# Attention and mixture of experts: five late slots of three blocks, early buffers, and the next x turned in quarters

## The chip, the cores and the metric

The kernel runs on one core of a Trainium2 chip. The time is the device time of one execution, in microseconds, taken as the median of several runs. The profile is of one further execution; its engines are TensorE (PE, with PEld for the loading of the stationary operand), VectorE (DVE), ScalarE (ACT), GpSimd (POOL) and SyncE (SP), which issues most of the DMA transfers.

## The reference

An attention over 32 memory rows a head makes x, and a mixture of eight experts works on x. Each token goes to the one expert with the largest gate logit.

```python
a = softmax(phi, axis=sequence)              # batch 8, heads 8, sequence 576, memory 32
k_m, v_m = a^T k, a^T v                      # per head: 32 x 64
attn = softmax(q k_m^T / 8) v_m              # 8 x 8 x 576 x 64
x = attn as 4608 tokens x 512
e_idx = argmax(x @ w_gate)                   # 512 x 8
out[t] = prob[t, e] * sigmoid(x @ w_output_gate)[t, e] * (relu(x[t] @ w1[e]) @ w2[e])
                                             # w1: 8 x 512 x 1024, w2: 8 x 1024 x 512
```

Everything is float32. The counts of tokens of the experts follow from the data, and the kernel finds them at run time.

## The kernel before

**Attention.** The eight batches are worked as four pairs. For each pair a generator `memory` makes the memory rows (18 pauses long in its written order MEM), and the queries go in five chunks a pair, 20 in all. The loop over `t` in `attention` does one step for each chunk, and some more for its lag: the list ORDER says in which order the parts of a step are issued, and each part works on the chunk that its lag gives. X is the exponential (ACT, L796), S the transpose, the maximum and the shift (DVE L787 and L790, POOL L792), D the division, B the transpose back, V0 and V1 the values (PE L825, copy on ACT L827, store on SP L936 and L940), C the scores of the next chunk (PE L779), M and m a pause's worth of `memory`, R a number of pauses of the routing. Each engine works its instructions in the order in which they are issued here.

**Routing.** After each pair, `rank` finds the expert of each token and its place among that expert's tokens. After the second pair `route_early(0)`, after the third `route_early(1)`, after the last `route_late` turn counts into a plan of slots. A slot is up to three blocks of 128 tokens of one expert. Two plus three early slots of three (NPS) take full triples only; then come NPT late slots of three, NPP of two, and up to NSS of one, which run in branches only if the counts ask for them (`used`). A slot's expert is in the table `slot` (read by SP), its rows in the lists `idx_ga`, `idx_gb` (slots 2 to 4) and `idx_gl` (the late ones), DVE L238. `known` marks slots whose expert is there, `listed` those whose rows are.

**Experts.** `run` works the slots in order. The rows are gathered from `xs` in HBM (POOL L480), turned by TensorE against the identity into a PSUM bank (`turn_x`, L988), and split into a high part (ACT L989) and a low part (DVE L990). A slot's weights are eight units of 512 KB: four of w1 (L1117), four of w2 (L1136). Each is loaded (SP L507) into a buffer of the ring `raw`, and split into high (ACT L518) and low (DVE L519) into the ring `ring`. Every product is taken three times (high by high, low by high, high by low). Relu and its split are ACT L1122 and DVE L1123, the scaled result ACT L1096, its scatter POOL L1097. After each unit, `done` splits as many units ahead as the ring allows.

**How the two are interleaved.** At the part S of step 19 (START) the slots begin, and the rest of the attention and the late routing are issued from `hook` in `several`, two entries of ORDER or two pauses at a time: twice a unit in u=0 to 3, and once for each block of a unit in u=4 to 7. Before the slots begin the rings have three raw buffers, two split ones and one for gathered rows. `grow(0)` adds two to each, in memory that the attention's pools `qk` and `ld` leave when they are closed; `grow(1)` adds the rest after slot 1 (LAST, `settle`). PSUM has four banks for the slots until then, and six afterwards; the results of w2 hold three of them from u=4.

Of the kernel before, what the change touches and what calls it, by code (L numbers as in the profile page):

```python
# [7 lines left out]
F32 = mybir.dt.float32  # L8
# [4 lines left out]
ALU = mybir.AluOpType  # L13
# [3 lines left out]
P = 128  # L17
B, H, S, D, M = 8, 8, 576, 64, 32
# [7 lines left out]


NPS = (2, 3)
NPT, NPP, NSS = 6, 4, 19
NPE = sum(NPS)  # L30
NB3, NB2 = 3 * NPT, 2 * NPP
NBL = NB3 + NB2 + NSS
NSLOT = NPE + NPT + NPP + NSS
NTHR = 13

ORDER = ["R4", "X", "S", "R0", "m", "D", "M", "B", "V0", "R1", "R1", "V1", "M", "m", "C"]
LAG = {"X": 1, "B": 2, "D": 1, "V": 3, "C": -1}
TICK = 0
HOOK = (2, 2, 2, 2, 2, 2)
# [13 lines left out]
LATE = {"lg": 8, "w": 2, "pe": 0, "dve": 0}  # L53
GROW = ((2, 2, 2), (6, 1, 0))
PUMP = (2, 1)
LAST = 1
XQ = 144
XROW = 4 * XQ
# [6 lines left out]
def attention_moe(tc, phiT, kv, qT, wgo, wall, out):  # L65
    nc = tc.nc
    V, A, G, T = nc.vector, nc.scalar, nc.gpsimd, nc.tensor

    with contextlib.ExitStack() as ctx:
# [5 lines left out]
        ident = cp.tile([P, P], F32, name="ident")  # L75
# [387 lines left out]
        for s in range(NSLOT):  # L463
            nb = 3 if s < NPE + NPT else 2 if s < NPE + NPT + NPP else 1
            if s < NPE:
                k = s >= NPS[0]
# [7 lines left out]
        order = slots  # L474
# [497 lines left out]
                    self.step()  # L972
                return self.got

        def turn_x(z, c2):

            nb, xg = z["nb"], z["xg"]
            if c2 == 0:
                z["x"] = (mo.tile([P, 4, 3 * P], F32R, name="xh"), mo.tile([P, 4, 3 * P], F32R, name="xl"))
            xh, xl = z["x"]  # L980
            n = nb * P
            w = 1 if nb == 3 else 2
            for c in range(2 * c2, 2 * c2 + 2, w):
                pt = bank([w, 512 // w], "ps")
                for j in range(w):
                    for k in range(nb):
                        o = (c + j) * XQ
                        T.transpose(pt[:, j, k * P:(k + 1) * P], xg[:, k, o:o + P], ident[:])  # L988
                A.copy(xh[:, c:c + w, 0:n], pt[:, :, 0:n])  # L989
                V.tensor_tensor(xl[:, c:c + w, 0:n], pt[:, :, 0:n], xh[:, c:c + w, 0:n].bitcast(F32), ALU.subtract)  # L990

        NT = 5 * NBP
        deferred = []
# [18 lines left out]
        def attention():  # L1012

            nonlocal rou
            st, lgs = {}, {}
            while 0 not in kTs:
                mem.step()
            st[0] = scores(0, 0)
            load_q(NQ)
            xo = None  # L1020
            for t in range(NT + LAG["V"]):
                for w in ORDER:
                    g = t - LAG.get(w[0], 0)
                    if w in ("M", "m"):
                        if w == "M" or t % 5 < 4:
                            mem.step()
                    elif w[0] == "R":
                        rou.step(int(w[1:]))
                    elif w == "W":
                        if order[0]["known"] and stream.parted < ring.size:  # L1030
                            stream.split(ring.size)
                    elif w == "V0" and 0 <= g < NT:
                        bp, c = g // 5, g % 5
                        while 2 * bp + (c >= 2) not in ves:
                            mem.step()
                        if g == 5 * bp:
                            lgs[bp] = rt.tile([P, NCH, 16], F32, name="lg", bufs=2)
                        xo = wk.tile([P, 2, 2, 2 * XQ], F32, name="xo", bufs=2)
                        values(bp, 2 * c, st[g], xo)
                    elif w == "V1" and 0 <= g < NT:  # L1040
                        if c < 4:
                            values(bp, 2 * c + 1, st[g], xo)
                        store(bp, c, xo, lgs[bp])
                    elif w == "C" and 0 < g < NT:
                        while 2 * (g // 5) + (g % 5 >= 2) not in kTs:
                            mem.step()
                        st[g] = scores(g // 5, g % 5)
                        if g + NQ < NT:
                            load_q(g + NQ)
                    elif w == "S" and 0 <= g < NT:  # L1050
                        shift(st[g])
                    elif w == "X" and 0 <= g < NT:
                        expo(st[g])
                    elif w == "D" and 0 <= g < NT:
                        divide(st[g])
                    elif w == "B" and 0 <= g < NT:
                        back(st[g])
                    undefer()
                    clock[0] += 1
                    yield "open" if w == "S" and t == START else None  # L1060
                g = t - LAG["V"]
                if g >= 0 and g % 5 == 4:
                    bp = g // 5
                    undefer(99)
                    left.append(bp)
                    rou.finish()
                    if bp < NBP - 1:
                        rou = Side(rank(bp, lgs[bp]))
                    else:
                        late.gens.append(rank(bp, lgs[bp]))  # L1070
                if t == NT - 1:
                    mem.finish()
                    pm.close()
                    grow(0)
# [26 lines left out]
        def several(i, st, nxt, hook):  # L1101

            z = order[i]
            nb, x, h = z["nb"], z["x"], []
            n_ = nb * P
            for u in range(4):
                w = st.take(i, u)
                h_ = mo.tile([P, 2, 3 * P], F32R, name="hh", bufs=4)
                l_ = mo.tile([P, 2, 3 * P], F32R, name="hl", bufs=4)
                for j in range(2):  # L1110
                    if nb == 3 or j == 0:
                        pb = bank([1, 512] if nb == 3 else [2, 256], "ps")
                    n = 0
                    for cc in range(4):
                        for a, b in PASS:
                            o = cc * 256 + j * P
                            T.matmul(pb[:, j % pb.shape[1], 0:n_], w[:, b, o:o + P], x[a][:, cc, 0:n_],  # L1117
                                     start=(n == 0), stop=(n == 11))
                            n += 1
                    if nb == 3 or j == 1:  # L1120
                        js = slice(j, j + 1) if nb == 3 else slice(0, 2)
                        A.activation(h_[:, js, 0:n_], pb[:, :, 0:n_], AF.Relu)  # L1122
                        V.scalar_tensor_tensor(l_[:, js, 0:n_], pb[:, :, 0:n_], 0.0, h_[:, js, 0:n_].bitcast(F32),  # L1123
                                               ALU.max, ALU.subtract)
                    if j == 0:
                        hook()
                h.append((h_, l_))
                st.done(PUMP[0])
                hook()
            py = [bank([DM], "ps") for _ in range(nb)]  # L1130
            for u in range(4, 8):
                w = st.take(i, u)
                for k in range(nb):
                    for f in range(2):
                        for n, (a, b) in enumerate(PASS):
                            T.matmul(py[k], h[u - 4][a][:, f, k * P:(k + 1) * P], w[:, b, DM * f:DM * f + DM],  # L1136
                                     start=(u == 4 and f == 0 and n == 0), stop=(u == 7 and f == 1 and n == 2))
                    if u == 7:
                        finish_y(z, k, py[k])
                    hook()  # L1140
                if u in (4, 6):
                    nxt(u // 2 - 2)
                st.done(PUMP[0])

        def single(i, st, nxt):
# [16 lines left out]
            for u in range(4):  # L1162
# [12 lines left out]
                    turn_h(0)  # L1175
                if u < 3:
                    st.done(PUMP[1])
            nxt(0)
            nxt(1)
            turn_h(1)  # L1180
            st.done(PUMP[1])
            py = bank([DM], "ps")
# [22 lines left out]
        def run(st):  # L1205

            lo, hi = st.lo, st.hi // 8
            while not order[lo]["known"]:
                force()
            st.fetch()  # L1210
            if lo:
                gat[:] = lo, hi

            def hook():
                gathers(i)
                clock[0] += not att.gens
                (att if att.gens else late).step(HOOK[min(i, 5)])

            for i in range(lo, hi):
                gathers(i, i + 1)  # L1220
                if i == lo:
                    turn_x(order[i], 0)
                    turn_x(order[i], 1)

                def nxt(c2):
                    if i + 1 < hi:
                        gathers(i, i + 2)
                        turn_x(order[i + 1], c2)

                if order[i]["nb"] > 1:  # L1230
                    several(i, st, nxt, hook)
                else:
                    single(i, st, nxt)
                if i == LAST:
                    settle()
# [56 lines left out]
```

## Time and profile before

| | us |
|---|---|
| median of 3 runs | 670.93 (670.58 to 672.78) |
| the profiled execution's own time | 669.65 |
| its span, first to last instruction | 667.9 |
| mean granted TensorE clock | 0.937 |
| TensorE busy | 587.3 (88%) |
| VectorE busy | 354.5 (53%) |
| ScalarE busy | 285.4 (43%) |
| GpSimd busy | 166.2 (25%) |

The span is cut by the first matmul on w1 (L1117) of each slot. Attention and early routing lie ahead of 130.3 us; the 15 slots follow up to about 652 us; the last scatters and the check for single slots end it. A row of a view of stretches gives the stretch, its length, and for each engine its busy time with the number of instructions, then the granted clock (1.00 is full), the busy share of the DMA engines and GB/s. A row of a timeline gives start, duration, engine, line, operation, tiles and shapes, and in brackets how long the engine was idle before and what ended that.

### The profile page before, as it was taken

How to read it: one execution, taken by the hardware profiler on the slowest of the kernel's cores; microseconds unless marked ns; L12 is line 12 of the kernel's file. 1: busy time of each engine (PE TensorE's matmuls, PEld its weight loads, DVE VectorE, ACT ScalarE, POOL GpSimd, SP SyncE). 2: the span in 40 equal slices, each digit the busy share in tenths (PEclk: the TensorE clock that was granted, in tenths of full speed). 3: DMA queues.
4: the chain of work that ended last, by engine and by line, in shares of the span. 5: the costliest groups of instructions: out<-in, count | busy, mean ns of one | idle time of the engine just before them, and what ended most of it. 6: DMA issues, size and time to landing. Idle time of an engine off the chain costs nothing. (4 is left out here: it accounts for less than half of the span.)

```text
span 667.9 us, 11253 instructions
## 1 busy us (share of the span) xinstructions
PE 587.3 (88%) x4287; PEld 505.7 (76%) x4287; DVE 354.5 (53%) x706; ACT 285.4 (43%) x479; POOL 166.2 (25%) x198
## 2 busy tenths in 40 slices
PE   4588886577699889989999999999999999999990
PEld 3356563466479679888989898989898999899880
DVE  3668799744345559954444444444445353565410
ACT  4556654323235246423434353535343444555410
POOL 2334656402401441120304040303020212121101
PEclk9889688578799999989999999999999999999996
DMA  8999999313555749554645555464746363776000
GB/s 313 411 399 409 380 346 307 110 53 104 183 172 172 242 111 340 191 144 147 197 155 172 181 156 196 140 213 108 233 114 201 126 190 119 230 245 180 22 6 26
DMA packets 42911, 129.25 MB, mean 194 GB/s; under 512 B 9824, under 2 KB 9888, under 8 KB 42464
## 3 DMA queue, kind: packets, MB, share of 16 engines
q1 hardware_dynamic: 36288, 106.90, 49.2%
q0 software_dynamic: 6560, 21.54, 8.9%
q8 instruction: 36, 0.59, 0.3%
q14 instruction: 27, 0.22, 0.1%
HBM read 108.07 MB, written 21.66 MB: 194 GB/s over the span
## 5 line engine op out<-in xcount | busy, mean ns | idle before, releaser
L1117 PE MATMUL bps<-xh,whl 128*128 128x384 f32 (+1 forms) x960 | 235.8, 329 | 10.1 <-ACT whl L518 6.1
L1136 PE MATMUL bps<-whl,hh 128*128 128x512 f32 x656 | 215.2, 398 | 2.2 <-ACT whl L518 1.5
L519 DVE TENSOR_TENSOR whl<-w,whl 128x1024 fp32r<-128x1024 f32 x120 | 145.4, 1225 | 88.2 <-ACT whl L518 88.2
L1117 PEld LDWEIGHTS bps<-xh,whl 128*128 128x128 f32 x960 | 171.6, 193 | 14.5 <-ACT whl L518 7.4
L1117 PE MATMUL bps<-xl,whl 128*128 128x384 f32 (+1 forms) x480 | 156.7, 326 | 0.0
L1136 PEld LDWEIGHTS bps<-whl,hh 128*128 128x128 f32 x656 | 124.1, 189 | 29.0 <-ACT whl L518 1.8
L1136 PE MATMUL bps<-whl,hl 128*128 128x512 f32 x328 | 128.8, 393 | 0.0
L518 ACT CAST whl<-w 128x1024 fp32r<-128x1024 f32 x120 | 123.7, 1049 | 0.0
L1122 ACT ACTIVATE hh<-bps 128x384 fp32r<-128x384 f32 (+1 forms) x104 | 52.0, 509 | 112.8 <-PE bps L1117 112.8
L1123 DVE SCALAR_TENSOR_TENSOR hl<-bps,hh 128x384 fp32r<-128x384 f32 (+1 forms) x104 | 58.7, 575 | 70.1 <-ACT hh L1122 69.9
L1117 PEld LDWEIGHTS bps<-xl,whl 128*128 128x128 f32 x480 | 92.9, 193 | 0.5
L1097 POOL DMA_INDIRECT out<-y,idx_ol x26 | 32.0, 1231 | 234.5 <-ACT y L1096 205.4
L990 DVE TENSOR_TENSOR xl<-bps,xh 128x384 fp32r<-128x384 f32 (+1 forms) x52 | 28.6, 575 | 95.6 <-ACT xh L989 95.4
L989 ACT CAST xh<-bps 128x384 fp32r<-128x384 f32 (+1 forms) x52 | 24.2, 498 | 123.7 <-PE bps L988 123.7
L1136 PEld LDWEIGHTS bps<-whl,hl 128*128 128x128 f32 x328 | 62.2, 190 | 11.6
L1096 ACT ACTIVATE y<-bps,xg 128x512 f32<-128x512 f32 x41 | 28.2, 688 | 61.6 <-DMA out<-y,idx_ol 23.8
L988 PE MATMUL bps<-ident,xg 128*128 128x128 f32 x164 | 26.6, 292 | 10.9 <-DMA xg<-xs,idx_ga 5.2
L825 PE MATMUL bpd<-ve_b,aT 64*128 64x144 f32 (+1 forms) x320 | 31.7, 358 | 4.0 <-DVE ea L787 2.4
L988 PEld LDWEIGHTS bps<-ident,xg 128*128 128x128 f32 x164 | 21.0, 148 | 16.7 <-DVE xl L990 5.6
L827 ACT COPY xo<-bpd 128x576 f32<-128x576 f32 x36 | 22.5, 637 | 25.7 <-PE bpd L825 16.1
L480 POOL DMA_INDIRECT xg<-xs,idx_gl x26 | 27.9, 1072 | 18.8 <-DVE idx_ol L241 11.2
L825 PEld LDWEIGHTS bpd<-ve_b,aT 64*128 64x128 f32 (+1 forms) x320 | 24.3, 218 | 10.2 <-DVE ea L787 3.1
(232 smaller groups left out, 427.4 us busy)
## 6 DMA issues: line engine op xcount, KB each, us to landing
w<-wall SPq DMA_DIRECT2D x120, 512.0 KB, 4.3
kvt<-kv SPq DMA_DIRECT2D x32, 512.0 KB, 7.9
xs<-xo SPq DMA_DIRECT2D x16, 576.0 KB, 5.7
qt<-qT SPq DMA_DIRECT2D x16, 512.0 KB, 8.3
ph<-phiT SPq DMA_DIRECT2D x3, 1152.0 KB, 12.0
kv<-kv SPq DMA_DIRECT2D x4, 512.0 KB, 9.2
ph<-phiT SPq DMA_DIRECT2D x4, 288.0 KB, 3.9
xs<-xo SPq DMA_DIRECT2D x8, 144.0 KB, 3.9
```

The lines of the kernel that those rows point to most:

```text
L480: G.indirect_dma_start(out=z["xg"][:, k], out_offset=None, in_=xs[0:z["rows"]], in_offset=bass.IndirectOffsetOnAxis(ap=z["idx"][0][:, q:q ...
L518: A.copy(hl[:, 0], w[:])
L519: V.tensor_tensor(hl[:, 1], w[:], hl[:, 0].bitcast(F32), ALU.subtract)
L825: T.matmul(px[to:to + n, r, sl], z["aT"][h, o:o + n], ves[2 * bp + b][h, g], start=True, stop=True)
L988: T.transpose(pt[:, j, k * P:(k + 1) * P], xg[:, k, o:o + P], ident[:])
L990: V.tensor_tensor(xl[:, c:c + w, 0:n], pt[:, :, 0:n], xh[:, c:c + w, 0:n].bitcast(F32), ALU.subtract)
L1096: A.activation(y[:], py, AF.Copy, scale=z["xg"][:, k, P:P + 1])
L1097: G.indirect_dma_start(out=out, out_offset=bass.IndirectOffsetOnAxis(ap=z["idx"][1][:, z["q0"] + k:z["q0"] + k + 1], axis=0), in_=y[:], in ...
L1117: T.matmul(pb[:, j % pb.shape[1], 0:n_], w[:, b, o:o + P], x[a][:, cc, 0:n_], start=(n == 0), stop=(n == 11))
L1122: A.activation(h_[:, js, 0:n_], pb[:, :, 0:n_], AF.Relu)
L1123: V.scalar_tensor_tensor(l_[:, js, 0:n_], pb[:, :, 0:n_], 0.0, h_[:, js, 0:n_].bitcast(F32), ALU.max, ALU.subtract)
L1136: T.matmul(py[k], h[u - 4][a][:, f, k * P:(k + 1) * P], w[:, b, DM * f:DM * f + DM], start=(u == 4 and f == 0 and n == 0), stop=(u == 7 an ...
```

## The change

Three things are edited.

- NPT goes from 6 to 5, and NSS from 19 to 22. The lists keep 45 columns.
- In the attention: W joins ORDER behind R4. The loop already has a branch for it, which splits one weight unit if slot 0 is known and fewer units are split than the ring has buffers. The edit adds a second branch with the same condition further down the same chain of `elif`. And the closing of the pools `qk` and `ld` with `grow(0)` goes from the end of step 19 to the end of step 18.
- `turn_x` now turns one quarter of the next slot's x (one chunk of 128 columns; two at once where the slot has fewer than three blocks), and `several` calls it at four places of its second half instead of two halves behind u=4 and u=6. TURN gives the places, counted in blocks of units from u=4: for three blocks 1, 4, 6 and 9 of 12.

```diff
--- before.py
+++ after.py
@@ -26,14 +26,14 @@
 
 
 NPS = (2, 3)
-NPT, NPP, NSS = 6, 4, 19
+NPT, NPP, NSS = 5, 4, 22
 NPE = sum(NPS)
 NB3, NB2 = 3 * NPT, 2 * NPP
 NBL = NB3 + NB2 + NSS
 NSLOT = NPE + NPT + NPP + NSS
 NTHR = 13
 
-ORDER = ["R4", "X", "S", "R0", "m", "D", "M", "B", "V0", "R1", "R1", "V1", "M", "m", "C"]
+ORDER = ["R4", "W", "X", "S", "R0", "m", "D", "M", "B", "V0", "R1", "R1", "V1", "M", "m", "C"]
 LAG = {"X": 1, "B": 2, "D": 1, "V": 3, "C": -1}
 TICK = 0
 HOOK = (2, 2, 2, 2, 2, 2)
@@ -53,6 +53,7 @@
 LATE = {"lg": 8, "w": 2, "pe": 0, "dve": 0}
 GROW = ((2, 2, 2), (6, 1, 0))
 PUMP = (2, 1)
+TURN = {3: (1, 4, 6, 9), 2: (1, 2, 4, 5)}
 LAST = 1
 XQ = 144
 XROW = 4 * XQ
@@ -972,22 +973,24 @@
                     self.step()
                 return self.got
 
-        def turn_x(z, c2):
+        def turn_x(z, c):
+
 
             nb, xg = z["nb"], z["xg"]
-            if c2 == 0:
+            if c == 0:
                 z["x"] = (mo.tile([P, 4, 3 * P], F32R, name="xh"), mo.tile([P, 4, 3 * P], F32R, name="xl"))
             xh, xl = z["x"]
             n = nb * P
             w = 1 if nb == 3 else 2
-            for c in range(2 * c2, 2 * c2 + 2, w):
-                pt = bank([w, 512 // w], "ps")
-                for j in range(w):
-                    for k in range(nb):
-                        o = (c + j) * XQ
-                        T.transpose(pt[:, j, k * P:(k + 1) * P], xg[:, k, o:o + P], ident[:])
-                A.copy(xh[:, c:c + w, 0:n], pt[:, :, 0:n])
-                V.tensor_tensor(xl[:, c:c + w, 0:n], pt[:, :, 0:n], xh[:, c:c + w, 0:n].bitcast(F32), ALU.subtract)
+            if c % w:
+                return
+            pt = bank([w, 512 // w], "ps")
+            for j in range(w):
+                for k in range(nb):
+                    o = (c + j) * XQ
+                    T.transpose(pt[:, j, k * P:(k + 1) * P], xg[:, k, o:o + P], ident[:])
+            A.copy(xh[:, c:c + w, 0:n], pt[:, :, 0:n])
+            V.tensor_tensor(xl[:, c:c + w, 0:n], pt[:, :, 0:n], xh[:, c:c + w, 0:n].bitcast(F32), ALU.subtract)
 
         NT = 5 * NBP
         deferred = []
@@ -1029,6 +1032,10 @@
                     elif w == "W":
                         if order[0]["known"] and stream.parted < ring.size:
                             stream.split(ring.size)
+                    elif w == "W":
+
+                        while t == NT - 1 and stream.split(2):
+                            pass
                     elif w == "V0" and 0 <= g < NT:
                         bp, c = g // 5, g % 5
                         while 2 * bp + (c >= 2) not in ves:
@@ -1068,7 +1075,7 @@
                         rou = Side(rank(bp, lgs[bp]))
                     else:
                         late.gens.append(rank(bp, lgs[bp]))
-                if t == NT - 1:
+                if t == NT - 2:
                     mem.finish()
                     pm.close()
                     grow(0)
@@ -1138,8 +1145,9 @@
                     if u == 7:
                         finish_y(z, k, py[k])
                     hook()
-                if u in (4, 6):
-                    nxt(u // 2 - 2)
+                    step = nb * (u - 4) + k
+                    if step in TURN[nb]:
+                        nxt(TURN[nb].index(step))
                 st.done(PUMP[0])
 
         def single(i, st, nxt):
@@ -1175,8 +1183,8 @@
                     turn_h(0)
                 if u < 3:
                     st.done(PUMP[1])
-            nxt(0)
-            nxt(1)
+            for c in range(4):
+                nxt(c)
             turn_h(1)
             st.done(PUMP[1])
             py = bank([DM], "ps")
@@ -1219,13 +1227,13 @@
             for i in range(lo, hi):
                 gathers(i, i + 1)
                 if i == lo:
-                    turn_x(order[i], 0)
-                    turn_x(order[i], 1)
-
-                def nxt(c2):
+                    for c in range(4):
+                        turn_x(order[i], c)
+
+                def nxt(c):
                     if i + 1 < hi:
                         gathers(i, i + 2)
-                        turn_x(order[i + 1], c2)
+                        turn_x(order[i + 1], c)
 
                 if order[i]["nb"] > 1:
                     several(i, st, nxt, hook)
```

## The prediction

> **What bounds the kernel now.** I read the page first, then TensorE's work in stretches cut at the first L1117 matmul of each slot, then its waits.
>
> ```profile
> span 667.9 us, 11253 instructions
> PE 587.3 (88%) x4287; PEld 505.7 (76%) x4287; DVE 354.5 (53%) x706; ACT 285.4 (43%) x479; POOL 166.2 (25%) x198
> ```
>
> ```profile
> core 0: us, PE busy (x) PEld busy (x) DVE busy (x) ACT busy (x) POOL busy (x), PEclk, DMA share, GB/s
> 130.26:198.77 68.51, 52.08 (x229) 41.28 (x229) 28.36 (x70) 19.13 (x29) 13.11 (x15) 0.83 0.39 121
> 198.77:240.29 41.52, 37.72 (x237) 32.76 (x235) 22.11 (x65) 16.63 (x27) 13.93 (x17) 1.00 0.56 180
> ...
> 490.40:524.80 34.40, 34.40 (x182) 31.40 (x180) 15.60 (x20) 14.87 (x23) 5.87 (x5) 1.00 0.53 163
> 524.80:558.80 34.00, 34.00 (x178) 30.97 (x176) 14.94 (x18) 14.30 (x21) 5.88 (x5) 1.00 0.53 165
> ```
>
> These are slots 0, 1, 9 and 10. The late triples run with TensorE busy all the time at full clock, 34.40 us each; the last takes 34.00, since a pair behind it needs fewer transposes. DVE, ACT and the DMA engines are about half used there. So from slot 4 on TensorE's own work sets the time. Slot 0 takes twice as long, and there waits set it:
>
> ```profile
> PE bps L1117 <- ACT whl L518: 6.1, 4, 1.5
> PE bps L988 <- DMA xg<-xs,idx_ga: 5.2, 3, 4.7
> PE bps L988 <- DVE xl L990: 2.3, 2, 1.2
> PE bps L1117 <- DVE whl L519: 2.2, 4, 0.6
> PE bps L1136 <- ACT whl L518: 1.5, 1, 1.5
> PE bps L1136 <- DVE whl L519: 0.7, 1, 0.7
> ```
>
> The columns are the total, the times and the longest. They sum to 18.0 us: weights that are split only when they are wanted, the gather of slot 1, and the second transpose of a pair of chunks.
>
> **The slot that goes.** I computed the routing from the reference's inputs. Experts get 576, 576, 0, 0, 576, 1152, 1152 and 576 tokens. After the five early slots they have 2, 2, 0, 0, 2, 6, 6 and 5 blocks left. That is five triples (0+0+0+2+2+1), four pairs and no single: exactly what five and four slots hold. The sixth triple is then empty in the kernel before, and the trace can tell. Software-queue traffic in 523.0 to 540.0 (three scatters of slot 9 and two gathers), then in 557.0 to 572.0 (three scatters of slot 10 and two gathers), in packets and MB:
>
> ```profile
> q0 software_dynamic: 326, 1.12, 17.7%
> q0 software_dynamic: 291, 0.22, 6.6%
> ```
>
> The second set of scatters moves almost no bytes. NPT is the number of late triples, so the edit drops one run of 34.40 us: its 96 and 72 matmuls, its splits, gathers and weights, all off the engine that sets the end. The table has 15+8+22 = 45 columns against 18+8+19 = 45, so the routing tables keep their size; three more single slots lengthen a few small DVE operations in late routing, which I cost at nothing, since DVE is busy 15.60 of 34.40 us. **Term: -34.4 us**, bounds -34.0 and -34.4.
>
> **The first weights, split in the attention.** The branch that runs is the one already there, the first with that name: it does at most one split a step, as soon as slot 0 is known. Counting the generator's yields, that is known in step 15 (first R1). In step 16, R4 fetches three weights, and W, directly behind it, puts the ACT copy and the DVE subtraction of the first weight into their queues, ahead of that step's exponential (L796) and transpose (L787). The rows:
>
> ```profile
> 105.25 0.63 ACT L796 ACTIVATE ea<-ea 128x512 f32<-128x512 f32 x1 [0.80 <-POOL ea L792]
> 107.66 1.45 SPq L507 DMA_DIRECT2D w<-wall  x3
> 107.71 0.71 DVE L787 STREAM_TRANSPOSE ea<-bpd 128x512 f32<-128x512 f32 x1
> ```
>
> ```profile
> w<-wall SPq DMA_DIRECT2D x1, 512.0 KB, 4.4
> ```
>
> ```profile
> 129.16 1.05 ACT L518 CAST whl<-w 128x1024 fp32r<-128x1024 f32 x1
> 130.24 1.23 DVE L519 TENSOR_TENSOR whl<-w,whl 128x1024 fp32r<-128x1024 f32 x1 [0.39 <-ACT whl L518]
> 130.26 0.69 PE L1117 MATMUL bps<-xh,whl 128*128 128x384 f32 x1 [1.51 <-ACT whl L518]
> ```
>
> ```profile
> 107.71:125.43 17.72, 16.41 (x45) 0.65 0.76 236
> ```
>
> The first weight lands 4.4 us after 107.66, at 112.1. ACT copies to 113.1; DVE, 1.08 us behind and 1.23 long, ends at 114.4. The transpose that stood at 107.71 starts at 114.4: **6.7 us later**. Queued behind on ACT are the exponential (at 105.25 before), the K copies and L827; behind on DVE the rest of step 16. The last row (DVE between this transpose and the last one, length and busy time) says that DVE works 16.41 of 17.72 us up to slot 0, so at most 1.3 us is caught up; I take 0. On SP the fourth weight's load waits for the first's buffer, up to 114.4, with the step's store behind it. Two more splits (steps 17 and 19) add 2 x 1.23 = **2.5 us** to DVE; their ACT copies (1.05 each) lie in ACT's idle time. What goes is the wait of **1.5 us** before the first matmul. So slot 0's first matmul moves from 130.26 to 130.26 + 6.7 + 2.5 - 1.5 = **137.9** (bounds 130.0, if the stall is absorbed, and 144, if SP's held stores delay the attention by as much again).
>
> **Buffers and quarters in slot 0.** With the rings grown one step earlier, four split weights and five raw ones stand ready, and slot 1's gather is issued at the start of slot 0. The attention's memory part has 18 pauses a pair of batches and is through by step 16, so finishing it at step 18 moves nothing. Of the 18.0 us of waits all should go: the splits run three ahead, the gather has half a slot, and a quarter's three transposes have 18 matmuls to the next. What stays is the half clock:
>
> ```profile
> 113.10:137.00 23.90, 15.57 (x126) 0.50 0.44 136
> ...
> 140.40:143.80 3.40, 2.92 (x9) 0.50 0.53 153
> ...
> 150.60:154.00 3.40, 3.40 (x16) 0.51 0.55 154
> ...
> 174.50:184.80 10.30, 7.52 (x24) 0.50 0.25 76
> ```
>
> TensorE's busy time and clock are the second and third number. From 130.26 to 137.0 it works some 6.5 us at half clock, later 2.9, 3.4 and 7.5: 20.3 us, half of it lost, 10.2. Slot 0 without waits and slow clock is 68.5 - 18.0 - 10.2 = 40.3 us. The clock was still low 6.7 us behind the first matmul, after a sparse attention; I keep that, 3.4 us lost. **Slot 0: 43.7 us** (bounds 42 and 50), so slot 1 starts at 181.6, not 198.77.
>
> **The new wait in slot 1.** Here the edit costs. Each W is an entry more in a step, and the rest of the attention goes two entries per hook. The list of slot 2's rows (idx_gb, L238) was in entry 52 behind the start, hook 26, the end of u=2 in slot 1. With three more W's it is entry 55, hook 28, the end of u=3. And the first transposes of slot 2 move from behind u=4 to its second of three parts. Before:
>
> ```profile
> 212.88 0.56 DVE L1123 SCALAR_TENSOR_TENSOR hl<-bps,hh 128x384 fp32r<-128x384 f32 x1 [1.52 <-ACT hh L1122]
> 213.81 1.23 DVE L519 TENSOR_TENSOR whl<-w,whl 128x1024 fp32r<-128x1024 f32 x1 [0.38 <-ACT whl L518]
> 214.96 0.17 DVE L238 TENSOR_SCALAR idx_gb<-iv 128x9 int32<-128x9 f32 x1
> ...
> 217.91 0.56 DVE L1123 SCALAR_TENSOR_TENSOR hl<-bps,hh 128x384 fp32r<-128x384 f32 x1 [1.44 <-ACT hh L1122]
> ```
>
> ```profile
> 215.39 1.05 POOL L480 DMA_INDIRECT xg<-xs,idx_gb  x1 [7.36 <-DVE i L239]
> ...
> 218.07 1.00 POOL L480 DMA_INDIRECT xg<-xs,idx_gb  x1 [0.31 <-issue]
> ```
>
> ```profile
> 217.19 0.39 PE L1136 MATMUL bps<-whl,hh 128*128 128x512 f32 x1
> ...
> 222.71 0.33 PE L988 MATMUL bps<-ident,xg 128*128 128x128 f32 x1 [0.41 <-DMA xg<-xs,idx_gb]
> ```
>
> ```profile
> DMA to landing us min/median/max: 4.6/5.2/5.8
> ```
>
> L238 starts 2.1 us behind the start of the unit's last L1123, the first gather 0.4 later. One unit on, L1123 starts 0.7 us behind the end of u=3 (217.91 against 217.19), so the gathers start 3.2 us behind it; the third starts 2.7 later and lands 4.6 on: 10.5 us behind it. TensorE arrives after 12 of the 18 matmuls that took 217.19 to 221.3, so after 2.7 us, and stands some **7.6 us** (bounds 0 and 8). Queued behind those transposes is all of TensorE's work. The waits of slot 1 before, by its rows,
>
> ```profile
> PE bps L988 <- DVE xl L990: 2.3, 2, 1.2
> PE bps L988 <- DMA xg<-xs,idx_gb: 0.8, 2, 0.4
> ```
>
> go (3.1 us). The stand will lower the clock as the gather's did at 174.5 to 184.8, which cost 7.5/2 = 3.8 us; without that one's second stalls I take **3 us** (bounds 0 and 5).
>
> The Trainium skill, "TensorE: Matmul & The Clock Gate", section "What's actually happening", says that one idle window of about 3.4 us halves the clock and about 3.4 us of sustained work restores it; by that the slow phase costs an estimated 1.7 us in place of 3, and the sum falls by 1.3 us. The 10.3 us row here is three such windows, so the trace speaks for more.
>
> Slot 1: 41.52 - 3.1 + 7.6 + 3 = **49.0 us**; it ends at 181.6 + 49.0 = 230.6, not 240.29. **Term: -9.7 us.** Slots 2 and 3 keep their work and their waits, late routing being only one or two hooks later with a slot to spare; later slots have no wait that quarters could take away. The store of the last rows is unchanged.
>
> **Sum.** The profiled execution took 669.65 us around its span of 667.9. 669.65 - 34.4 - 9.7 = 625.6. The median of the runs, 670.93, is 1.3 above it: **626.8 us**.
>
> **The rivals.**
>
> *The early part comes through whole (23%).* The wait in slot 1 is covered, because POOL and DVE get ahead: 626.8 - 10.6 = **616**; with 1.3 caught up and a shorter slow clock at the start, 613. For it: POOL idles 7.36 us before that gather. Against: L238 is behind a DVE instruction that needs u=3.
>
> *The early part brings nothing (24%).* The split that waits for its weight holds ACT, DVE and SP at once; with the held stores the attention's buffers come free late, and slot 0 starts 8 to 10 us later than I say: 670.93 - 34.4 = **636.5**. For it: DVE works 16.41 of 17.72 us there. Against: attention's stores are few, and the DMA share at that place is 0.76.
>
> *Slower: five triples do not suffice (3%).* One place, the count of late blocks: from the sixth full triple on, its three blocks go to single slots, in the branches behind the last pair, with nothing fetched ahead. A single has 48 matmuls of half a weight's width and 24 of 512 columns, by slot 9's rate 11 us, with transposes 13. Two branches start cold, with list, weight (4.4), split (2.3) and gather (5.2): some 12 us each. 3 x 13 + 2 x 12 = 63 us against the 34.4 saved: 626.8 + 63 = **690**. Against: the counts above, and the two q0 rows.
>
> *It does not do what it says.* The second branch named W stands behind an equal condition and never runs. If it were the one that counts, all splits would stand in step 19, no weight would be waited for, and the sum would be 6.7 lower, 620; that lies inside the range and gets no chance of its own.
>
> **How the numbers follow.** My forecast gets 50%, at 620 to 632; the rivals 23, 24 and 3. The range is 613 to 638: it takes in both neighbours and leaves out two tails. A difference under 0.3% (2 us) can't be told from none here. All cases but the slower one are faster by far more: faster 0.96, same 0.01, slower 0.03.
>
> **What would show it.** Right: 14 slots, the late ones still 34.40 us; the first L518 in front of an L796 near 112, DVE idle some 5 us before it; slot 0's first matmul near 138 and its length near 44, no wait for whl; a wait of TensorE for idx_gb near 7 us in slot 1, with half clock behind it. Wrong: a first matmul before 132 or after 143, no such wait, a whl wait in slot 0, or any single slot.

## The result and the profile after

The changed kernel takes 617.35 us (median of 4 runs, 616.07 to 618.26) against 670.75 for the kernel before: a ratio of 0.920, 95% interval 0.917 to 0.923. The forecast was 626.8, so the direction and most of the size were right, and some 9 us more were gained than I had worked out. The time lies inside the range of 613 to 638, but below the 620 to 632 of my own case. The profiled execution took 618.26 us around a span of 616.6; the sum had been made for that, and gave 625.6. So 7.3 us of the miss lie in the terms below, and the rest in how the medians stand to the profiled executions.

The page of the changed kernel, its first two lines:

```profile
span 616.6 us, 10779 instructions
PE 541.8 (88%) x4107; PEld 467.0 (76%) x4107; DVE 344.2 (56%) x686; ACT 273.2 (44%) x456; POOL 160.1 (26%) x192
```

TensorE has 180 matmuls fewer, which is 12 + 96 + 72: one slot of three. The view of stretches, cut again at the first w1 matmul of slots 0 to 3 and of a late slot (the line of that matmul is now L1124, of the w2 matmuls L1143):

```profile
139.42:178.78 39.36, 39.36 (x222) 34.06 (x221) 25.53 (x69) 17.82 (x29) 10.73 (x14) 0.99 0.53 156
178.78:225.67 46.89, 40.16 (x243) 34.27 (x242) 21.39 (x59) 16.85 (x27) 9.40 (x10) 0.93 0.53 160
225.67:260.20 34.53, 34.53 (x181) 31.31 (x180) 30.99 (x79) 20.82 (x29) 16.10 (x15) 1.00 0.76 260
260.20:300.52 40.32, 38.00 (x217) 34.41 (x216) 24.68 (x44) 15.23 (x23) 6.88 (x6) 0.96 0.52 164
404.10:438.63 34.53, 34.53 (x182) 31.31 (x180) 16.17 (x20) 15.24 (x23) 7.11 (x6) 1.00 0.56 171
```

| | before, us | after, us | difference | forecast |
|---|---|---|---|---|
| first w1 matmul | 130.26 | 139.42 | +9.2 | +7.6 |
| slot 0 | 68.51 | 39.36 | -29.1 | -24.8 |
| slot 1 | 41.52 | 46.89 | +5.4 | +7.5 |
| slot 2 | 36.61 | 34.53 | -2.1 | 0 |
| slot 3 | 41.50 | 40.32 | -1.2 | 0 |
| a late slot of three | 34.40 | none | -34.4 | -34.4 |
| the five others from slot 4 on, 34.53 for 34.40, and the end | | | +1.0 | 0 |

The differences sum to -51.2, and the spans differ by 51.3. Slot 0 is fully busy: its stretch and TensorE's busy time are the same 39.36 us.

The step in which the first weight is split, on ACT, DVE and SP (timelines of the changed kernel; L519 and L520 are the two halves of a split, L508 the load):

```profile
109.23 7.09 SPq L508 DMA_DIRECT2D w<-wall  x4
```

```profile
113.66 1.04 ACT L519 CAST whl<-w 128x1024 fp32r<-128x1024 f32 x1 [7.45 <-DMA w<-wall]
114.61 0.62 ACT L797 ACTIVATE ea<-ea 128x512 f32<-128x512 f32 x1
```

```profile
109.06 0.18 DVE L295 TENSOR_TENSOR q<-q,q 128x18 f32<-128x18 f32 x1
114.74 1.23 DVE L520 TENSOR_TENSOR whl<-w,whl 128x1024 fp32r<-128x1024 f32 x1 [5.50 <-ACT whl L519]
115.88 0.71 DVE L788 STREAM_TRANSPOSE ea<-bpd 128x512 f32<-128x512 f32 x1
```

The same operation of DVE in the kernel before, where the transpose comes 0.10 us behind its start, at 107.71:

```profile
107.61 0.18 DVE L294 TENSOR_TENSOR q<-q,q 128x18 f32<-128x18 f32 x1
```

ACT stands 7.45 us for the weight, with the exponential right behind it. DVE stands 5.50 us and works 1.23 before the transpose. Without them the transpose would have started at 109.06 + 0.10 = 109.16; it starts at 115.88, 6.7 us later. SP holds four loads over 7.09 us, the last until the first buffer is free.

And the wait in slot 1, in the waits of TensorE over that slot and in its timeline, with the list of rows (DVE) and the gathers (POOL):

```profile
PE bps L991 <- DMA xg<-xs,idx_gb: 6.5, 3, 6.0
```

```profile
200.79 0.17 DVE L239 TENSOR_SCALAR idx_gb<-iv 128x9 int32<-128x9 f32 x1
```

```profile
201.23 1.05 POOL L481 DMA_INDIRECT xg<-xs,idx_gb  x1 [17.14 <-DVE idx_ob L242]
```

```profile
197.99 0.39 PE L1143 MATMUL bps<-whl,hh 128*128 128x512 f32 x1
...
206.94 0.45 PE L991 MATMUL bps<-ident,xg 128*128 128x128 f32 x1 [6.03 <-DMA xg<-xs,idx_gb]
...
208.33 0.47 PE L991 MATMUL bps<-ident,xg 128*128 128x128 f32 x1 [0.27 <-DMA xg<-xs,idx_gb]
```

u=4 begins at 197.99, the list comes 2.8 us later, the first gather 3.2 us later and the last transpose 10.3 us later; the forecast had 2.8, 3.2 and 10.5.

### The profile page after: what moved, and what is told of

Its sections match the earlier page's. It is cut to its first block, busy times and chain, and to the rows that moved or that the text cites. A ratio compares the mean times of both kernels' runs of the same rounds, so it can differ in the third digit from the quotient of the medians.

```text
span 616.6 us, 10779 instructions
## 1 busy us (share of the span) xinstructions
PE 541.8 (88%) x4107; PEld 467.0 (76%) x4107; DVE 344.2 (56%) x686; ACT 273.2 (44%) x456; POOL 160.1 (26%) x192
## 5 line engine op out<-in xcount | busy, mean ns | idle before, releaser
L1124 PE MATMUL bps<-xh,whl 128*128 128x384 f32 (+1 forms) x896 | 214.1, 322 | 0.0
L1143 PE MATMUL bps<-whl,hh 128*128 128x512 f32 x608 | 204.2, 401 | 0.0
L520 DVE TENSOR_TENSOR whl<-w,whl 128x1024 fp32r<-128x1024 f32 x112 | 137.0, 1230 | 76.3 <-ACT whl L519 76.2
L1124 PEld LDWEIGHTS bps<-xh,whl 128*128 128x128 f32 x896 | 157.2, 190 | 1.1 <-issue 0.2
L1124 PE MATMUL bps<-xl,whl 128*128 128x384 f32 (+1 forms) x448 | 143.9, 321 | 0.0
L1143 PEld LDWEIGHTS bps<-whl,hh 128*128 128x128 f32 x608 | 115.0, 189 | 23.4
L519 ACT CAST whl<-w 128x1024 fp32r<-128x1024 f32 x112 | 116.2, 1045 | 10.1 <-DMA w<-wall 8.1
L1143 PE MATMUL bps<-whl,hl 128*128 128x512 f32 x304 | 119.2, 392 | 0.0
L1124 PEld LDWEIGHTS bps<-xl,whl 128*128 128x128 f32 x448 | 85.3, 190 | 0.5
L1104 POOL DMA_INDIRECT out<-y,idx_ol x23 | 24.2, 1053 | 212.0 <-ACT y L1103 183.5
L1143 PEld LDWEIGHTS bps<-whl,hl 128*128 128x128 f32 x304 | 57.7, 190 | 10.4
L793 POOL TENSOR_TENSOR ea<-ea,mx 128x512 f32<-128x512 f32 (+1 forms) x20 | 19.2, 959 | 48.6 <-DVE mx L791 48.6
```

What stands on the lines that cost most here:

```text
L519: A.copy(hl[:, 0], w[:])
L520: V.tensor_tensor(hl[:, 1], w[:], hl[:, 0].bitcast(F32), ALU.subtract)
L1104: G.indirect_dma_start(out=out, out_offset=bass.IndirectOffsetOnAxis(ap=z["idx"][1][:, z["q0"] + k:z["q0"] + k + 1], axis=0), in_=y[:], in ...
```

## The experiments

My theory is that four things move separately: the empty slot, the buffers handed over early, the quarters, and the entry W, which costs twice (a weight that ACT and DVE wait for, and three entries that put a list one unit later). Each run below takes one of them away or does it alone.

**The slots alone.** The kernel before with one edit.

```diff
-NPT, NPP, NSS = 6, 4, 19
+NPT, NPP, NSS = 5, 4, 22
```

> The kernel before with five late triples and 22 singles, nothing else. My theory: the sixth triple is empty and TensorE-bound, so the time falls by its 34.4 us and nothing else moves: 636.4 us, first w1 matmul at 130 us, slots 0 and 1 near 68 and 41 us. Rival: part of the 34.4 us is given back, because the last slots then wait for weights or rows: 645 us or more, with waits of TensorE in the late slots.

Measured: 635.56 us (634.96 to 639.03) against 670.17, ratio 0.950 (0.946 to 0.955): 34.6 us less. Slots 0 and 1 take 64.65 and 42.62 us, near the kernel before; a late slot is unchanged and TensorE waits in none:

```profile
421.73:456.11 34.38, 34.38 (x181) 31.39 (x180) 15.70 (x20) 14.89 (x23) 6.96 (x6) 1.00 0.54 172
```

So the slot's own length is the gain, and nothing is given back. The other 18 us belong to the rest of the change.

**Without W.** The changed kernel with the list ORDER of before.

```diff
-ORDER = ["R4", "W", "X", "S", ...
+ORDER = ["R4", "X", "S", ...
```

> The changed kernel without the entry W: no weight is split inside the attention. My theory: W costs more than it brings. First w1 matmul back at 130 to 131 us, one wait of some 2 us for the second unit in slot 0, none afterwards, slot 0 at 43 to 46 us; the list of slot 2 comes two hooks earlier, so the wait for its rows falls from 6.5 to 2 to 4 us; together 606 to 609 us. Rival: the early splits are what made slot 0 short: slot 0 at 55 us or more, 617 us or more.

Measured: 610.15 us (608.86 to 611.36), ratio 0.910 (0.907 to 0.914). W makes the kernel about 7 us slower. The first matmul comes at 132.82, slot 0 takes 46.05 us and slot 1 38.99. Waits of TensorE in slot 0 and, last row, in slot 1:

```profile
PE bps L1124 <- ACT whl L519: 3.0, 2, 1.5
PE bps L1124 <- DVE whl L520: 0.9, 2, 0.6
```

```profile
PE bps L991 <- DMA xg<-xs,idx_gb: 1.6, 3, 0.8
```

Two units wait for their split where I had one (the first of the slot and the second); then the splits run ahead. So the rings, not W, keep slot 0 fed after its second unit. The time is a little above what I expected, and so are the first matmul and slot 0.

**W that counts as no entry.** The split stays where it is; the loop goes on to the next part without a pause and without moving the clock of the delayed parts.

```diff
+                    if w == "W":
+                        continue
                     undefer()
                     clock[0] += 1
```

> The changed kernel in which W splits as before but does not count as an entry for the hooks. My theory, that three more entries put the list of slot 2 one unit later: first w1 matmul stays at 139 us, the wait for the rows of slot 2 falls from 6.5 to 1 to 3 us and the half clock behind it goes, 610 to 613 us. Rival, that the wait comes from slot 0 being faster than the attention behind it: the wait stays over 5 us and the time within 2 us of 617.

Measured: 611.08 us (610.69 to 612.39), ratio 0.912 (0.909 to 0.916), 6 us better than the change. The first matmul stays at 138.84, slot 0 at 40.01 without a wait; slot 1 falls from 46.89 to 39.19 us, at full clock:

```profile
178.85:218.04 39.19, 37.38 (x236) 32.56 (x235) 22.78 (x70) 16.21 (x27) 14.09 (x16) 1.00 0.59 189
```

```profile
PE bps L991 <- DMA xg<-xs,idx_gb: 1.8, 3, 0.8
```

Slot 0 is as fast as in the change, so it isn't its speed that makes the wait: the three entries do.

**W in step 19 only.** The first of the two branches is taken out, so that the second runs.

```diff
-                    elif w == "W":
-                        if order[0]["known"] and stream.parted < ring.size:
-                            stream.split(ring.size)
```

> The changed kernel without the first of the two branches named W, so that the second one runs: two splits in step 19, when their weights have long landed. My theory, that ACT and DVE waited for a weight in step 16: no such wait, first w1 matmul at 132 to 134 us, the wait for the rows of slot 2 unchanged near 6.5 us, 610 to 613 us. Rival, that something else holds the end of the attention (rows, the scores, POOL): first w1 matmul at 137 us or later, the time within 2 us of 617.

Measured: 609.92 us (609.31 to 611.21), ratio 0.911 (0.908 to 0.914). ACT does the two copies at 125.12 without waiting for a weight, the first matmul comes at 131.43, slot 0 takes 40.27 us without a wait, and the wait in slot 1 is still there:

```profile
125.12 1.98 ACT L519 CAST whl<-w 128x1024 fp32r<-128x1024 f32 x2
```

```profile
131.43:171.70 40.27, 40.27 (x222) 34.98 (x221) 26.55 (x70) 18.68 (x30) 10.77 (x14) 0.97 0.55 173
```

```profile
PE bps L991 <- DMA xg<-xs,idx_gb: 6.2, 3, 5.8
```

The first matmul is 8.0 us earlier than in the change, which is the stall and one split (6.7 + 1.2). The other price of W, the wait in slot 1, is untouched, so the two are separate.

**Halves in place of quarters.**

```diff
-                    step = nb * (u - 4) + k
-                    if step in TURN[nb]:
-                        nxt(TURN[nb].index(step))
+                if u in (4, 6):
+                    nxt(u - 4)
+                    nxt(u - 3)
```

> The changed kernel with the next x turned in two halves behind u=4 and u=6, as in the kernel before. My theory: in slots 0 and 1, which have one spare bank of PSUM, each half waits once for the split of its first chunk (1.2 us each, 2.3 a slot); the first half of slot 1 stands one part of a unit later, so the wait for the rows of slot 2 falls by 1.4 to 5 us; slot 2's wait for y (1.9 us) comes back; late slots shorter by 0.1 us each: 619 to 622 us. Rival, that the quarters bring nothing: within 1 us of 617, no wait for the split of x in slot 0.

Measured: 622.89 us (620.09 to 625.07) against 669.01, ratio 0.930 (0.926 to 0.933), some 5.5 us slower than the change and a little over what I expected. Waits of slot 0 (first row), then of slots 1 and 2:

```profile
PE bps L991 <- DVE xl L993: 2.4, 2, 1.2
```

```profile
PE bps L991 <- DMA xg<-xs,idx_gb: 4.7, 2, 4.5
PE bps L1124 <- ACT y L1103: 2.2, 1, 2.2
PE bps L991 <- issue: 1.5, 2, 1.2
PE bps L991 <- DVE xl L993: 1.2, 1, 1.2
```

The wait for y is in slot 2, the others of this view in slot 1. The waits that the quarters took away come back, the one for y with them, and a late slot is at 34.39 us again.

**The buffers handed over at the end of step 19**, as before.

```diff
-                if t == NT - 2:
+                if t == NT - 1:
```

> The changed kernel with the buffers handed over at the end of step 19, inside slot 0, as before. My theory: two or three units of slot 0 wait some 2.2 us each for their split, and slot 1's rows come late (wait of 3 to 5 us), with half clock behind these: slot 0 at 48 to 54 us in place of 39.4, time 626 to 632 us. Rival, that the early hand-over is not what made slot 0 short: slot 0 under 43 us, time within 2 us of 617.

Measured: 636.45 us (632.64 to 636.76), ratio 0.949 (0.945 to 0.954). Right in kind, and larger than I said: slot 0 takes 62.16 us, not 48 to 54.

```profile
PE bps L991 <- DMA xg<-xs,idx_ga: 7.6, 3, 7.0
PE bps L1124 <- ACT whl L519: 3.0, 2, 1.5
PE bps L1143 <- ACT whl L519: 1.5, 1, 1.5
PE bps L1124 <- DVE whl L520: 1.3, 2, 0.6
PE bps L1143 <- DVE whl L520: 0.5, 1, 0.5
```

The rows of slot 1 come 7.6 us late, where I had 3 to 5, and the clock is halved three times in the slot. The time is that of the slots alone (0.949 against 0.950): without the early buffers, W and the quarters together bring nothing that these runs can tell. One thing goes the other way, and I had not expected it: slot 0 begins at 135.47, 4.0 us earlier than in the change. 1.2 us of this are the third split, for which two split buffers leave no room in the attention, and 1.6 the load, issued at 107.67; the rest is not followed up.

**Both costs of W avoided.** No entry W; where the slots begin, two units are split once, ahead of the first x.

```diff
-ORDER = ["R4", "W", "X", "S", ...
+ORDER = ["R4", "X", "S", ...
...
                 if i == lo:
+                    while i == 0 and st.split(2):
+                        pass
                     for c in range(4):
                         turn_x(order[i], c)
```

> The changed kernel without the entry W; instead the first two units are split once, where the slots begin, ahead of the transposes of the first x. My theory: no wait for a weight on ACT, no entry more for the hooks, so both costs go and the gain stays: first w1 matmul at 129 to 132 us, slot 0 at 40 us without a wait, a wait of 1.5 to 3 us for the rows of slot 2, 600 to 603 us. Rival, that the two splits on DVE hold the first x's low parts: first w1 matmul at 134 us or later, 606 us or more.

Measured: 606.83 us (604.67 to 607.48), ratio 0.907 (0.904 to 0.911). Faster than the change, and 4 us slower than I expected. The time is one that the rival named (606 or more), but its sign, a first matmul at 134 or later, is absent. The first matmul is at 131.95 and slot 0 takes 39.88 us, as expected, but slot 1 takes 40.63:

```profile
PE bps L991 <- DMA xg<-xs,idx_gb: 1.7, 3, 0.7
PE bps L1124 <- DVE xl L993: 1.1, 1, 1.1
```

The second row is what the rival named, DVE's two splits ahead of the first x's low part, at 1.1 us. The profiled execution is the fastest of the four, 604.67; the rest of the miss is not settled. Taken apart, the two prices of W brought 6.3 and 7.4 us; avoided together they bring 10.5.

**The same, with the quarters later.**

```diff
-TURN = {3: (1, 4, 6, 9), 2: (1, 2, 4, 5)}
+TURN = {3: (3, 5, 7, 9), 2: (1, 2, 4, 5)}
```

> The kernel of the run before with the quarters two parts of a unit later (3, 5, 7 and 9 of 12). My theory: the wait for the rows of slot 2 goes, and the last quarter still has 12 matmuls before the next slot: 1.5 to 3 us less than the run before, 598 to 601 us. Rival, that quarters this close wait for each other's bank or for the split of x: the same time as the run before or more, with such waits in slots 0 and 1.

Measured: 603.17 us (602.19 to 606.24), ratio 0.903 (0.898 to 0.907), the fastest kernel of the study, some 14 us under the change. That is 2 us above what I expected. Slot 1 falls to 37.59 us with no wait for rows. In slot 2 the wait for y is back (first row; the second stands ahead of slot 0's first matmul, the third in slot 1):

```profile
PE bps L1124 <- ACT y L1103: 1.5, 1, 1.5
PE bps L1124 <- DVE xl L993: 1.1, 1, 1.1
PE pr L246 <- DVE ohc L868: 0.7, 1, 0.7
```

Its interval overlaps that of the run before, so the 3.7 us between their medians are not shown to be a difference; against the change (0.917 to 0.923) it is clear.

## Why the prediction was right, and where it was off

**The slot that goes: right.** -34.4 us forecast, 34.6 measured alone.

**The first weights in the attention: right, in its mechanism and its size.** The stall of 6.7 us was measured as 6.7. The first matmul came at 139.42 in place of 137.9; the load had been issued 1.6 us later in this execution (109.23 against 107.66). That need not be the change's doing: without W it was issued anywhere from 107.66 to 110.20.

**Buffers and quarters in slot 0: right in the waits, off in the clock.** All waits went. The step that failed is "The clock was still low 6.7 us behind the first matmul, after a sparse attention; I keep that, 3.4 us lost": the granted clock was full again 0.6 us behind the first matmul, as these stretches show (length, busy time and clock are the first three numbers).

```profile
136.94:139.99 3.05, 3.05 (x14) 0.50 0.84 318
140.00:141.00 1.00, 1.00 (x8) 1.00 0.83 244
```

So 0.3 us were lost, not 3.4, and that is most of the 4.3 us by which slot 0 was sized too long. I took the ramp from the one profile of the kernel before, and the change did not visibly shorten it. With the slots alone TensorE stands the same 1.51 us for its first weight, and yet the clock is full 0.8 us ahead of the first matmul. With W in step 19 and with the late buffers it doesn't stand there, and the clock is full only 2.6 and 2.9 us behind it. So some 3 of the 29 us that slot 0 lost are not shown to come from the change. Part of the other 1.2 us is work that I had left in slot 0 and that the three entries put into slot 1: TensorE has 222 operations in slot 0 here, and 230 in 40.01 us where W is no entry.

**The new wait in slot 1: right, and somewhat too dear.** 6.5 us in place of 7.6. By its own rows the forecast should have said 7.8 (10.5 less 2.7). From TensorE's arrival at 200.92 to the last transpose at 208.33 it is 7.4 us, and the first two transposes in between, 0.45 us each, count as work. Of the clock I had taken 3 us.

```profile
204.80:211.60 6.80, 4.19 (x11) 0.50 0.79 258
```

Half of 4.19 us is 2.1. The estimate of 1.7 us from the Trainium skill, "TensorE: Matmul & The Clock Gate", section "What's actually happening", was nearer to it than mine; the slow phase of 6.8 us is two of that page's windows here, where the 10.3 us row of before had three.

**"Slots 2 and 3 keep their work and their waits": wrong by 3.3 us.** The wait for y (1.9 us) was gone in slot 2, and the wait for the late list in slot 3 fell from 3.6 to 2.3 us. The waits of TensorE over slots 2 and 3 before,

```profile
PE pr L226 <- DVE bwl L218: 3.6, 2, 2.7
PE bps L1117 <- ACT y L1096: 1.9, 1, 1.9
```

and after:

```profile
PE pr L227 <- DVE bwl L219: 2.3, 2, 1.5
```

The first hangs on where the quarters stand: it is there with halves (1.9 and 2.2 us) and with the later quarters (1.5), and in none of the six runs with the places 1, 4, 6 and 9. That the next slot then finds another PSUM bank free is my reading of it and wasn't tested apart.

**The rivals.** "The early part comes through whole" named the measured time (616), but not for its reason: the wait in slot 1 wasn't covered. "The early part brings nothing" (636.5) needed a slot 0 that begins 8 to 10 us later than I said; it began 1.5 us later. No single slot ran.

The pieces, each from one run: the slot -34.6 us; the early buffers -19 (636.45 to 617.35); the quarters -5.5 (622.89 to 617.35); W +7.2 (610.15 to 617.35). They sum to -52, where -53.4 was measured; they need not add up, since each of the last three was taken from the full change; the two prices of W above don't.

## What to carry to other kernels

Where work is interleaved by counting entries, an added entry moves everything counted behind it: look for a list or a gather that then comes after its reader. Work put ahead of a queue in order costs the wait for its own input, so split or copy early only what has landed; here two splits in step 19, in place of the first two in steps 16 and 17, met weights that had long landed, and the first matmul came 8.0 us earlier. And find out what a padded plan really needs: the largest gain was a slot that held no rows.

## What the runs showed that I had not expected

The clock can come back on transposes alone. In the run with the split at the opening, TensorE does twelve of them and then stands; the granted clock is full before the first matmul of the slot:

```profile
128.05:131.20 3.15, 2.82 (x12) 0.50 0.87 329
131.20:131.95 0.75, 0.00 (x1) 1.00 0.79 142
```

In the kernel before, 2.8 us of the same transposes, an idle 1.5 us and 6.7 us of matmuls passed before it was full; over the ten profiles it is full from 0.8 us ahead of slot 0's first matmul to 6.7 us behind it. The changes of the clock that the prediction's rows show, 137.0, 140.4, 143.8, 150.6, 154.0, 174.5 and 184.8, all stand 3.4 us or a whole multiple of it apart. So where the work falls between those points may matter, but that wasn't tested, and what sets the difference stays open.

Quarters cost a little where nothing waits: a late slot takes 34.53 us with four groups of transposes among its matmuls, and 34.39 with two.
